# A long convolution with a gated output stage: block 1 moved behind block 0, the last chunks of the second stage reordered, two taps moved to ScalarE and GpSimd

## The chip, the cores and the metric

The kernel runs on one core of one Trainium2 chip. The metric is the time of one execution on the device in microseconds (us). The median of three runs of the kernel before is 949.27 us (947.81 to 949.87).

## The reference

For x of 8 batches, 6400 positions and 128 channels, and a filter h of 6400 positions and 128 channels, in float32:

```
Xf = rfft(x, n=2*S, axis=1);  Hf = rfft(h, n=2*S, axis=0)
y  = irfft(Xf * Hf, n=2*S, axis=1)[:, :S]        # causal long convolution, per channel
gate_pre = sum over k of conv_w[k] * y shifted by 4 - k positions   # 5 taps, per channel
out = (sigmoid(gate_pre) * (y @ w_val)) @ w_out
```

## The kernel before, in words

The kernel computes the convolution with a transform of its own, written as four sets of small matmuls, with N = 6400 = 100 x 64 positions. Forward: a transform over 100 points (`Forward.half`, weights `sd`, constants `r1_sb`, result into the tile `gy`). Second stage: 13 blocks of up to four frequencies (`s2_mm`, lines 318 to 332, constants `m2`, a ring of three slots), and behind each block the product with the filter's spectrum `h_sb`: `Product.mul_u` and `mul_t` on VectorE, `Product.add` on GpSimd (lines 350 to 371). Third stage: 16 groups of four channels, here called quads (`s3_quads`, lines 373 to 407; constants `r3_sb`, results into `dt`). Fourth: the inverse transform back to positions, `Chunk.s4`, chunk by chunk. A chunk is five of the 64 columns (chunk 60 has four), named by its first column: 0, 5, 10 up to 60.

Each chunk then passes through methods of `Chunk` (lines 433 to 555):

- `s4`: matmuls into one PSUM buffer; `copies`: ScalarE copies the result to `y`.
- The five taps of the gate, each adding scaled values into cells of the columns a to a + 4 and more. `init` (ScalarE) writes the tap that reaches a fresh column first. `keep` (ScalarE) scales tap 3 into a spare buffer `q`, and tap 2 into a buffer `r` if the chunk has one; `add` (GpSimd) adds `q` and `r` to the cells. `taps` (VectorE) adds the other taps, one `scalar_tensor_tensor` each; tap 2 is among them only if the chunk has no `r` (line 514).
- `project` (matmul with w_val), `sigm` (ScalarE), `gate` (VectorE), `output` (matmul with w_out), `store` (ScalarE copy, then a DMA on SP's queue).

The work of neighbouring batches is interleaved. In the loop over batches, line 643 runs the 16 quads of the third stage; in each quad the forward transform of the next batch (`fx.half`, into two PSUM buffers of `single()`) and steps of the chunks that the batch before left over, listed by `VALUE`, `OUTPUT` and line 632. Then line 693 runs up to 15 steps s that interleave the 13 blocks of the next batch's second stage (`s2`, `times`, two blocks in even steps and one in odd ones) with the chunks of this batch in the order `chs` (line 670). All instructions stay in program order on their engine.

What concerns the change:

- In step 0 the order on TensorE is: block 0 (line 697), transform of chunk 60 (line 699), output of a chunk left over (line 702), block 1 (line 704). `s2` also issues the load of the constants three blocks on (line 683, SP's queue), `times` the load of the spectrum four blocks on (line 690).
- The order of chunks, except in the last batch, is 60, 0, 35, 40, 45, 50, 55, 5, 10, 15, 20, 25, 30 (line 670). Chunks 25 to 55 are `late`: only `s4` and the copy are done here, and everything else in the next third stage. Chunks 10, 15 and 20 are `held`: their taps are done here, and projection, sigmoid, gate and output in the next third stage. In step s the chunk s is transformed and copied, chunk s - 1 gets its taps (VectorE), chunk s - 2 its additions (GpSimd), lines 725 to 728. Chunk 5 stands at place 7; its projection and sigmoid come in step 10, the gate at the end of step 10, the output in step 11. In step 10 the sigmoid is issued on ScalarE ahead of that step's `copies`.
- The chunks left over are handed to the next third stage in the order `cs` (line 737), so their steps of the same quad are issued in that order.
- `keep` picks `q` for chunks that are not late from four buffers `keeps`: two tiles `p_t` and the two halves of `h_sb[0]` (line 487).
- `fx.sums` (two GpSimd instructions, `sd<-x`, and a further x load on SP's queue) runs twice in the second stage, in steps 9 and 10 (line 735), unless the next batch is the last. Its first three loads are issued in step 5.
- Four PSUM buffers (`ps1`, line 612) serve `s4`, `project`, `output` and `fx.half`. Blocks and quads use two buffers of two banks each (`ps2`).

Of the kernel before, what the change touches and what calls it, by code (L numbers as in the profile page):

```python
# [17 lines left out]
N1 = 100  # L18
# [12 lines left out]
CH = 5  # L31
HEAD = (60, 4)
CHUNKS = [HEAD] + [(a, CH) for a in range(0, 60, CH)]
NCH = len(CHUNKS)
OUT_ORDER = CHUNKS[1:] + [HEAD]
LATE = 35
HELD = 10
WAIT = 25
BL = 2 * SB * C
M2B = 3  # L40
MH = 6
HB = 4
XB = 3
XH = 8
VALUE = {10: 0, 15: 1, 20: 2, 25: 4, 30: 5, 35: 6, 40: 8, 45: 10, 50: 12, 55: 14}
OUTPUT = {10: 2, 15: 3, 20: 4, 25: 6, 30: 7, 35: 8, 40: 9, 45: 11, 50: 13}
AHEAD = {
    0: (1, 0, 0), 1: (1, 0, 1), 4: (0, 0, 0), 5: (0, 0, 1), 7: (1, 1, 0), 8: (0, 1, 0),
    9: (0, 1, 1), 10: (0, 2, 0), 11: (0, 2, 1), 12: (1, 1, 1), 13: (1, 2, 0), 14: (1, 2, 1),
# [80 lines left out]
def longconv_moe(ctx: ExitStack, tc: tile.TileContext, x, h, r1, m2, r3, m4, w64, out):  # L130
# [26 lines left out]
    h_sb = [ring_at[M2B + i] for i in (2, 0, 1, 3)]  # L157
# [7 lines left out]
    p_t = [cp.tile([128, CH, N1], F32, name=f"p_{i}") for i in range(2)]  # L165
    keeps = p_t + [h_sb[0][:, i : i + CH * N1].rearrange("p (n t) -> p n t", t=N1) for i in (0, BL // 2)]
    rows = [t.rearrange("p a d n -> p (a d n)")[:, : CH * N1].rearrange("p (n t) -> p n t", t=N1) for t in sd_sb]
    hd = dp.tile([NKB, 128, 2 * SB * C], F32, name="hd")

    def weights():  # L170
# [69 lines left out]
    class Forward:  # L240


        def __init__(self, src, dst, xs=x_sb, o=0):
            self.src, self.dst, self.n, self.s, self.i, self.o = src, dst, 0, 0, 0, o
            self.xs = xs[o % len(xs) :] + xs[: o % len(xs)]
# [186 lines left out]
    class Chunk:  # L432


        def __init__(self, b, i, ch, defer):
            self.b, self.i, self.ch = b, i, ch
            a, n = ch
            self.defer = defer
            self.late = defer and WAIT <= a < HEAD[0]
            self.held = defer and HELD <= a < WAIT  # L440
            self.r = None
            self.y = yl[a][:, :n] if a >= LATE else held_y[a] if a >= HELD else dv[:, a : a + n, 0, :N1]

        def s4(self):
# [39 lines left out]
                self.p = self.y  # L484

        def keep(self):
            self.q = p_t[(self.ch[0] - HELD) // CH % 2] if self.late else keeps[(self.i + (self.i // 8 if self.defer else 1)) % 4]
            self.first(3, self.q, self.p)
            if self.r is not None:
                self.first(2, self.r, self.p)  # L490
# [129 lines left out]
    for b in range(B):  # L620
        nxt = b + 1 < B


        steps = collections.defaultdict(list)
        for c in pend:
            a = c.ch[0]
            if a == HEAD[0]:
                t = NS - 1
            else:
                t = VALUE[a]  # L630
            if c.late:
                k = (a - WAIT) // CH
                if not nxt:
                    c.r = rows[k % 3]
                steps[2 * k] += [lambda c=c: c.taps(range(2))]
                steps[2 * k + 1] += [lambda c=c: c.taps(range(2, 4)), c.add]
            steps[t] += [c.project]
            steps[t if a in OUTPUT else NS - 1] += [c.sigm, c.gate]
            if a in OUTPUT:
                steps[OUTPUT[a]] += [c.output]  # L640
                steps[OUTPUT[a] + 1] += [c.store]
        pend = [c for c in pend if c.ch[0] in (HEAD[0], HEAD[0] - CH)]
        for g in range(NS):
            e = s3_quads(4 * g)
            f = []
            if nxt:
                f = fx.half([single(), single()])
                fx.sums(nc.gpsimd)
            for u in e:
                u()  # L650
            if nxt and g in AHEAD:
                ahead(*AHEAD[g])
            for u in f:
                u(act)
            if b == 0:
                next(wgen, None)
                next(wgen, None)
                if g < 8:
                    m4_load(m4_rest[0], g % 2)
                    if g % 2:  # L660
                        m4_rest.pop(0)
            for u in steps[g]:
                u()
        if nxt:
            h_load(HB - 1)
        if b + 2 < B:
            fx = Forward(x[b + 2], gy)


        chs = CHUNKS if not nxt else sorted(CHUNKS, key=lambda c: (c != HEAD, c[0] > 0, c[0] < LATE))  # L670
        cs = [Chunk(b, i, ch, nxt) for i, ch in enumerate(chs)]
        jobs = collections.defaultdict(list)
        for i, c in enumerate(cs):
            if i and not c.late and not c.held:
                jobs[i + 3].append(c)
        if not nxt:
            jobs[NCH + 2].append(cs[0])
        pr = {}

        def s2(kb):  # L680
            if nxt and kb < NKB:
                pr[kb] = Product(kb)
                m2_load(kb + M2B)

        def times(kb):
            if kb in pr:
                pr[kb].mul_u()
                pr[kb].mul_t()
                pr.pop(kb).add()
                h_load(kb + HB)  # L690

        outs, at = [], 0
        for s in range(max(NCH, *jobs) + 2):
            kbs = list(range(at, min(at + 2 - s % 2, NKB))) if nxt else []
            at += len(kbs)
            if s == 0:
                s2(0)
            if s < 2:
                cs[s].s4()
            late = pend[s : s + 1]  # L700
            if late and s == 0:
                late[0].output()
            for kb in kbs[:1]:
                s2(kb + 1)
            if m4_rest:
                m4_load(m4_rest.pop(0))
            for c in jobs[s]:
                c.project()
            if 1 < s < NCH:
                cs[s].s4()  # L710
            for c in outs + late[: s]:
                c.output()
            for c in jobs[s]:
                c.sigm()
            for kb in kbs[:1]:
                times(kb)
            for kb in kbs[1:]:
                s2(kb + 1)
            if s < NCH:
                cs[s].copies()  # L720
            for c in outs + late:
                c.store(p_t[0][:, : c.ch[1]] if s == 0 or nxt and c.ch[0] == CH else None)
            for kb in kbs[1:]:
                times(kb)
            if 0 < s <= NCH and not cs[s - 1].late:
                cs[s - 1].taps()
            if 2 < s < NCH + 2 and not cs[s - 2].late:
                cs[s - 2].add()
            for c in jobs[s]:
                c.gate()  # L730
            outs = jobs[s]
            if b + 2 < B:
                if s == 5:
                    fx.load(XB)
                if s in (9, 10):
                    fx.sums(nc.gpsimd)
        pend = [cs[0]] + [c for c in cs if c.held or c.late]

# [44 lines left out]
```

## Time and profile before

| | us |
|---|---|
| median of 3 runs | 949.27 (947.81 to 949.87) |
| the profiled execution | 944.9 |
| its span | 943.1 |
| TensorE busy (matmuls) | 852.3 (90%) |
| VectorE busy | 746.0 (79%) |
| GpSimd busy | 579.0 (61%) |
| ScalarE busy | 510.3 (54%) |

The second stages start at 145.03, 251.38, 357.52, 466.65, 574.52, 683.84 and 793.31 us of the span, the third stages behind them at 199.14, 305.48, 411.60, 520.75, 629.05, 737.93 and 847.49.

How to read the rows: PE is TensorE, DVE VectorE, ACT ScalarE, POOL GpSimd, SP the queue that issues most DMAs. A row of the timeline gives the start in us from the span's start, the duration of the group in us, engine, line, operation, out<-in by the program's names, partitions x elements of the first instruction, the count, and in brackets the idle time of the engine ahead of it and what ended that. All lines are L117, that of the helper that records instructions, so groups are told apart by their tiles: `pt` is PSUM, `ring` holds the constants and spectra of the second stage and, later, `y`, cells and spare buffers of the chunks 10 to 30, `dt` those of the chunks 0 and 5 and the third stage's results, `gl` and `yl` those of the later chunks. On TensorE, `gy,ring` is a block (32 matmul records), `m_sb,dt` a chunk's transform (40 records), `r_sb,gy` a quad (64), `r_sb,sd` a forward half (32), and a row with `w_sb` a projection or an output (4). The chain of waits is the work that ended last, followed back from the end.

### The profile page before, as it was taken

To read this page: it belongs to the slowest core of one execution; us is meant where nothing else is said; L and a number is where in the kernel's file an instruction comes from. 1 tells how busy PE (TensorE), PEld (TensorE's weight loads), DVE (VectorE), ACT (ScalarE), POOL (GpSimd) and SP (SyncE) were. 2 spreads that over 40 slices of the span, in tenths; PEclk is the share of its full clock that TensorE was granted. 3 is DMA by queue.
4 is the path that set the end of the run, shared out by engine and by line. 5 is a ranking of instruction groups with operands and counts; after the bars stand their busy time and mean duration, and the time that the engine had idled before them with its cause. 6 is when DMAs were issued, how large, how long until landed. Compare 5 with 4: busy or idle time off the path is not lost. (4 is left out here: it accounts for less than half of the span.)

```text
span 943.1 us, 48025 instructions
## 1 busy us (share of the span) xinstructions
PE 852.3 (90%) x21360; PEld 679.1 (72%) x21360; DVE 746.0 (79%) x1041; ACT 510.3 (54%) x1222; POOL 579.0 (61%) x602
## 2 busy tenths in 40 slices
PE   7799669999999999998999999989999899999897
PEld 6699658865788568965688658865589657885563
DVE  5657658788897988888798878878787787979786
ACT  4532452278624873277624774168723685248776
POOL 5446645866477755775477764876458673864332
PEclk9999899999999999999999999999999999999999
DMA  8786547827494557826584466934586364921112
GB/s 260 255 294 230 191 155 267 298 82 216 152 322 133 167 191 238 277 81 189 164 306 152 148 194 200 312 110 153 165 284 207 114 192 149 324 88 47 66 56 97
DMA packets 79406, 177.42 MB, mean 188 GB/s; under 512 B 14048, under 2 KB 27360, under 8 KB 79200
## 3 DMA queue, kind: packets, MB, share of 16 engines
q1 hardware_dynamic: 67104, 152.33, 47.8%
q10 hardware_dynamic: 12096, 22.03, 7.9%
q8 instruction: 168, 2.75, 1.2%
q14 instruction: 38, 0.31, 0.1%
HBM read 141.56 MB, written 32.77 MB: 185 GB/s over the span
## 5 line engine op out<-in xcount | busy, mean ns | idle before, releaser
L117 POOL TENSOR_TENSOR gy<-gy,ring 128x512 f32<-128x512 f32 (+1 forms) x182 | 220.1, 1239 | 105.8 <-DVE ring L117 50.7
L117 PEld LDWEIGHTS pt<-r_sb,gy 64*64 64x64 f32 x8192 | 141.6, 136 | 107.3 <-issue 69.2
L117 DVE TENSOR_TENSOR dt<-pt,ring 128x496 f32<-128x496 f32 x256 | 159.7, 666 | 65.1 <-ACT dt L117 63.7
L117 PEld LDWEIGHTS pt<-m_sb,dt 128*64 128x64 f32 x4096 | 185.2, 136 | 28.8 <-issue 12.7
L117 PE MATMUL pt<-m_sb,dt 128*64 128x100 f32 x4096 | 193.0, 248 | 7.7 <-DVE ring L117 6.3
L117 PE MATMUL pt<-gy,ring 128*64 128x128 f32 x3008 | 189.1, 278 | 11.7 <-PE pt L117 4.2
L117 POOL TENSOR_TENSOR sd<-x 128x256 f32<-128x256 f32 x236 | 182.1, 801 | 26.2 <-issue 14.8
L117 ACT COPY ring<-pt 128x512 f32<-128x512 f32 (+2 forms) x216 | 129.2, 600 | 122.4 <-PE pt L117 58.0
L117 PEld LDWEIGHTS pt<-gy,ring 128*64 128x64 f32 x3008 | 175.0, 135 | 25.0 <-PE pt L117 13.3
L117 PE MATMUL pt<-r_sb,gy 64*64 64x64 f32 x8192 | 161.1, 225 | 19.9 <-issue 14.6
L117 PE MATMUL pt<-r_sb,sd 50*64 50x100 f32 x4608 | 137.8, 252 | 29.5 <-issue 20.0
L117 DVE TENSOR_TENSOR gy<-pt,ring 128x1024 f32<-128x1024 f32 (+1 forms) x99 | 116.9, 1181 | 54.5 <-PE pt L117 52.5
L117 DVE TENSOR_TENSOR ring<-pt,ring 128x1024 f32<-128x1024 f32 (+2 forms) x131 | 134.5, 1027 | 11.9 <-PE pt L117 2.7
L117 PEld LDWEIGHTS pt<-r_sb,sd 50*64 50x64 f32 x4608 | 114.1, 136 | 36.9 <-issue 26.9
L117 ACT COPY gy<-pt 128x400 f32<-128x400 f32 x248 | 110.6, 500 | 28.2 <-PE pt L117 27.0
L117 ACT COPY yl<-pt 128x500 f32<-128x500 f32 (+1 forms) x89 | 51.1, 574 | 128.8 <-PE pt L117 128.7
L117 POOL TENSOR_TENSOR gl<-gl,p 128x500 f32<-128x500 f32 (+1 forms) x46 | 54.1, 1177 | 103.9 <-DVE gl L117 68.7
L117 ACT COPY dt<-pt 128x16 f32<-128x16 f32 (+2 forms) x310 | 62.7, 255 | 85.8 <-PE pt L117 85.8
L117 DVE SCALAR_TENSOR_TENSOR gl<-yl,w_sb,gl 128x500 f32<-128x500 f32 (+1 forms) x107 | 92.9, 874 | 2.6 <-POOL gl L117 0.4
L117 PE MATMUL pt<-ring,w_sb 128*64 128x500 f32 x320 | 80.7, 599 | 6.9 <-DVE ring L117 6.8
L117 DVE SCALAR_TENSOR_TENSOR ring<-pt,w_sb,ring 128x500 f32<-128x500 f32 (+3 forms) x94 | 63.1, 671 | 5.7 <-ACT ring L117 1.3
L117 POOL TENSOR_TENSOR ring<-ring,p 128x500 f32<-128x500 f32 (+1 forms) x24 | 25.2, 1051 | 47.4 <-DVE ring L117 22.9
(62 smaller groups left out, 794.0 us busy)
## 6 DMA issues: line engine op xcount, KB each, us to landing
ring<-m SPq DMA_DIRECT2D x69, 512.0 KB, 5.9
ring<-hd SPq DMA_DIRECT2D x63, 512.0 KB, 5.0
x<-xl SPq DMA_DIRECT2D x118, 256.0 KB, 3.3
ring<-hd ACTq DMA_DIRECT2D x42, 256.0 KB, 3.1
ring<-m ACTq DMA_DIRECT2D x42, 256.0 KB, 3.7
out<-ring SPq DMA_DIRECT2D x40, 250.0 KB, 3.8
out<-yl SPq DMA_DIRECT2D x40, 250.0 KB, 3.2
hd<-ring SPq DMA_DIRECT2D x8, 512.0 KB, 4.8
```

Of the source, the lines that this page charges most:

```text
L117: return self._tc.keep_in_program_order(call(*args, **kwargs))
```

## The change

Block 1 is issued directly behind block 0 in step 0. The last chunks come in the order 5, 10, 25, 15, 20, 30. Chunks 10 and 15 get a buffer `r`, in the two halves of `h_sb[3]`, so that their tap 2 is made by ScalarE (`first`, one activation) and GpSimd (`add`, one addition of 128 x 500) and not by VectorE. The buffers `q` are named by a table, `KEEP`, which gives each chunk the buffer that it had. The two `fx.sums` move from steps 9 and 10 to steps 7 and 8. Since the left-over chunks follow the order `cs`, chunk 25 also stands ahead of 15 and 20 in the third stage. The last batch keeps its order.

```diff
+ORDER = (60, 0, 35, 40, 45, 50, 55, 5, 10, 25, 15, 20, 30)
+KEEP = {0: 1, 5: 3, 10: 1, 15: 2, 20: 3}
...
+    seconds = {
+        a: h_sb[HB - 1][:, i : i + CH * N1].rearrange("p (n t) -> p n t", t=N1) for a, i in ((10, 0), (15, BL // 2))
+    }
...
-            self.r = None
+            self.r = seconds.get(a) if defer else None
...
         def keep(self):
-            self.q = p_t[(self.ch[0] - HELD) // CH % 2] if self.late else keeps[(self.i + (self.i // 8 if self.defer else 1)) % 4]
+            a = self.ch[0]
+            if self.late:
+                self.q = p_t[(a - HELD) // CH % 2]
+            else:
+                self.q = keeps[KEEP[a] if self.defer else (self.i + 1) % 4]
...
-        chs = CHUNKS if not nxt else sorted(CHUNKS, key=lambda c: (c != HEAD, c[0] > 0, c[0] < LATE))
+        chs = CHUNKS if not nxt else [(a, CH) if a < HEAD[0] else HEAD for a in ORDER]
...
             if s == 0:
                 s2(0)
+                s2(1)
             if s < 2:
                 cs[s].s4()
...
             for kb in kbs[:1]:
-                s2(kb + 1)
+                if kb:
+                    s2(kb + 1)
...
-                if s in (9, 10):
+                if s in (7, 8):
                     fx.sums(nc.gpsimd)
```

## The prediction

> **What bounds the kernel now.** I read the page first: its chain of work that ended last.
>
> ```profile
> PE 27%; DVE 6%; issue 4%; ACT 2%; DMA 1%; POOL 1%; SPq 0%; DVEq 0%; POOLq 0%; ACTq 0%
> ```
>
> TensorE (PE) leads the chain and VectorE (DVE) is second, so an edit is worth what it takes from TensorE's waits, no more. The timeline shows them; I follow the batch whose second stage starts at 466.65 us. First TensorE and VectorE at the head of that stage:
>
> ```profile
> 468.55 1.54 PE L117 MATMUL pt<-m_sb,dt 128*64 128x100 f32 x32
> 469.93 0.83 PE L117 MATMUL pt<-gl,w_sb 128*64 128x400 f32 x4
> 470.60 3.86 PE L117 MATMUL pt<-gy,ring 128*64 128x128 f32 x64
> 474.29 1.90 PE L117 MATMUL pt<-m_sb,dt 128*64 128x100 f32 x40
> ```
>
> ```profile
> 472.69 1.23 DVE L117 TENSOR_TENSOR gy<-pt,ring 128x1024 f32<-128x1024 f32 x1 [1.42 <-PE pt L117]
> 473.95 1.23 DVE L117 TENSOR_TENSOR ring<-pt,ring 128x1024 f32<-128x1024 f32 x1
> 475.09 1.22 DVE L117 TENSOR_TENSOR gy<-pt,ring 128x1024 f32<-128x1024 f32 x1
> ```
>
> The first row is the inverse transform of chunk 60, the second its output projection, the 64 matmuls are blocks 1 and 2. VectorE sits idle 1.42 us until block 1 is there, then runs without a gap, and later TensorE waits for it or for what hangs on it:
>
> ```profile
> 485.06 2.07 PE L117 MATMUL pt<-gy,ring 128*64 128x128 f32 x32 [0.74 <-DVE dt L117]
> ...
> 489.28 2.07 PE L117 MATMUL pt<-gy,ring 128*64 128x128 f32 x32 [0.44 <-PE pt L117]
> ```
>
> Then TensorE at the end of the stage, where the transforms of chunks 20 and 25, the output of chunk 5, the transform of chunk 30 and the third stage follow one another:
>
> ```profile
> 512.71 1.94 PE L117 MATMUL pt<-m_sb,dt 128*64 128x100 f32 x40 [0.23 <-DVE ring L117]
> 515.13 1.94 PE L117 MATMUL pt<-m_sb,dt 128*64 128x100 f32 x40 [0.48 <-DVE ring L117]
> 518.05 1.06 PE L117 MATMUL pt<-dt,w_sb 128*64 128x500 f32 x4 [0.97 <-DVE dt L117]
> 518.93 1.89 PE L117 MATMUL pt<-m_sb,dt 128*64 128x100 f32 x40
> 520.75 1.19 PE L117 MATMUL pt<-r_sb,gy 64*64 64x64 f32 x64
> ```
>
> Three waits, 1.68 us, all for VectorE, whose rows say why: seven taps in one run, the gate of chunk 5 only behind them, then three taps of chunk 20 and 2.59 us of idleness before the third stage.
>
> ```profile
> 510.16 1.41 DVE L117 SCALAR_TENSOR_TENSOR dt<-pt,w_sb,dt 128x500 f32<-128x500 f32 x2 [0.58 <-ACT ring L117]
> ...
> 512.15 5.26 DVE L117 SCALAR_TENSOR_TENSOR ring<-pt,w_sb,ring 128x200 f32<-128x200 f32 x7
> 517.32 0.67 DVE L117 TENSOR_TENSOR dt<-pt,dt 128x500 f32<-128x500 f32 x1
> 517.91 2.28 DVE L117 SCALAR_TENSOR_TENSOR ring<-pt,w_sb,ring 128x500 f32<-128x500 f32 x3
> 522.78 1.26 DVE L117 TENSOR_TENSOR dt<-pt,ring 128x496 f32<-128x496 f32 x2 [2.59 <-ACT dt L117]
> ```
>
> **Part 1: block 1 directly behind block 0.** Nothing is added. Block 1 takes the place that chunk 60 had, near 468.5. Its data reached VectorE 472.69 - 470.60 = 2.09 us after its first matmul; so it is ready at 470.6, before VectorE is free at 472.69 - 1.42 = 471.27, and VectorE starts on it there, 1.42 us sooner. Block 2 gains nothing on TensorE, for the same work stands ahead of it: it starts half of (474.29 - 470.60) after 470.60, at 472.45, and is ready at 474.54. VectorE got to it at 475.09. The gain that VectorE keeps is thus 0.55 us. What is late next are the two waits above, 0.74 + 0.44 = 1.18 us, enough to take 0.55 in. The load of block 4's constants stands behind block 1 on SP's queue and goes out earlier; no queue entry is passed by another. Chunk 60's transform and output come later by one block; VectorE needs them only after block 2, so block 2's multiplications cover that. This happens ahead of seven third stages: 7 x 0.55 = 3.85 us.
>
> **Part 2: two taps leave VectorE, chunk 25 moves up.** Two taps of 2.28 / 3 = 0.76 us, one of chunk 10 and one of chunk 15, become each one activation and one addition. ScalarE and GpSimd (POOL) have rows for both, and for the two sums that move:
>
> ```profile
> 511.02 0.71 ACT L117 ACTIVATE p<-pt,w_sb 128x500 f32<-128x500 f32 x1
> ...
> 513.33 0.63 ACT L117 ACTIVATE dt<-dt 128x500 f32<-128x500 f32 x1
> 514.69 0.57 ACT L117 COPY ring<-pt 128x500 f32<-128x500 f32 x1 [0.73 <-PE pt L117]
> 515.16 1.44 ACT L117 ACTIVATE ring<-pt,w_sb 128x500 f32<-128x500 f32 x2
> ```
>
> ```profile
> 508.31 3.90 POOL L117 TENSOR_TENSOR gy<-gy,ring 128x512 f32<-128x512 f32 x4 [1.06 <-PE pt L117]
> 512.40 0.61 POOL L117 TENSOR_TENSOR dt<-dt,ring 128x200 f32<-128x200 f32 x1 [0.19 <-ACT ring L117]
> ...
> 515.85 1.42 POOL L117 TENSOR_TENSOR sd<-x 128x256 f32<-128x256 f32 x2
> 517.55 1.25 POOL L117 TENSOR_TENSOR ring<-ring,p 128x500 f32<-128x500 f32 x1 [0.28 <-DVE ring L117]
> ```
>
> Chunk 25 needs only a copy by ScalarE here, no VectorE. With it in the third place the transform of chunk 20 writes where chunk 25 stood, so the wait of 0.48 goes; the wait of 0.23, for chunk 5's taps, stays and now meets chunk 15.
>
> The gate of chunk 5 no longer has five taps of chunks 10 and 15 ahead of it, but two. Its sigmoid, however, gets a new wait. On GpSimd the two pairs of sums of the next batch now stand ahead of chunk 5's addition (512.40, 0.61 us): 508.31 + 3.90 + 2 x 1.42 = 515.05, so the addition ends at 515.66 and the sigmoid, before at 513.33, runs from 515.7 to 516.3. Behind it on ScalarE is queued all that chunks 15, 20 and 30 need. The gate then ends at 516.3 + 0.67 = 517.0, and chunk 5's output starts at 517.0 instead of 518.05. So the third stage starts 1.05 us earlier on TensorE, at 519.7.
>
> VectorE does not come along. Taps on a PSUM buffer start when ScalarE has finished reading it: at 510.16 they follow a wait for "ACT ring". ScalarE's steps follow each other at 0.47 us (514.69 to 515.16) to 0.7 us (half of 1.44), here taken as 0.56 for unhindered ones. From 516.2 it has seven: copy, first, keep and the new activation for chunk 15, then copy, first and keep for chunk 20: 3.9 us, to 520.1. The three taps of chunk 20 then last to 522.4, where they ended at 517.91 + 2.28 = 520.19 before. The join of the first quad, at 522.78 before, starts at 522.4: 0.4 us earlier. The 2.59 us of idle time was the cover for ScalarE's longer row, and it is used up. The x loads, two on SP behind the sums, go earlier, with nothing but the output of chunk 5 queued behind them; the new row buffers lie in the spectrum slot of block 11, which GpSimd releases at 510.8 (two of its four operations), before ScalarE gets there near 511.6. I cost these at nothing.
>
> **Where the 1.05 us goes.** In the third stage VectorE is late from the first quad to the sixth, and TensorE meets that at one place:
>
> ```profile
> 524.79 2.06 DVE L117 SCALAR_TENSOR_TENSOR ring<-ring,w_sb 128x500 f32<-128x500 f32 x2
> ...
> 528.52 0.73 DVE L117 SCALAR_TENSOR_TENSOR ring<-ring,w_sb 128x500 f32<-128x500 f32 x1
> ...
> 539.77 0.67 DVE L117 TENSOR_TENSOR ring<-pt,ring 128x500 f32<-128x500 f32 x1
> ```
>
> ```profile
> 537.92 0.87 PE L117 MATMUL pt<-r_sb,sd 50*64 50x100 f32 x32
> 540.49 1.06 PE L117 MATMUL pt<-ring,w_sb 128*64 128x500 f32 x4 [1.70 <-DVE ring L117]
> ```
>
> The projection of chunk 30 waits 1.70 us for the gate of chunk 25 (539.77, ends at 540.44), because the four single PSUM buffers are handed out in the order of their release and it gets that gate's buffer. The new order of chunks lists chunk 25 ahead of 15 and 20 in the third stage too, so its projection is issued ahead of chunk 20's output. Followed through the same rule, the gate's buffer now goes to the forward half of the sixth quad (537.92, 0.87 us), which TensorE reaches before chunk 30's projection. That half can no longer run during the wait: about 0.8 us of it falls behind the gate. If the gate moves by s, the projection moves by s + 0.8. With s = -0.4 that is +0.4: the lead of 1.05 is gone, and 0.4 with it.
>
> **The sum.** Six boundaries lead to third stages with forward halves: 6 x (0.4 - 0.55) = -0.9 us. The seventh leads into the last batch: no forward halves, no moved sums, hence no late sigmoid. There the last two waits go whole, 0.48 + 0.97 = 1.45, and part 1's 0.55: -2.0. Together -2.9 us. The profiled execution took 944.9 us (span 943.1 and 1.8 around it), 4.4 below the median of 949.27. I take the difference from the median: 946.4 us. With s from -1.0 (a ScalarE row shorter by 0.6) to 0 (a longer one) the sum runs from -6.5 to -0.5, so the forecast's own range is 942.8 to 948.8.
>
> VectorE's taps in the third stage read SBUF twice, and their price varies: 0.73 us for the one at 528.52, but 2.06 for the two at 524.79. In the sum I leave them as they are, though GpSimd's additions now end later. The Trainium skill, SBUF — State Buffer, section "Who interferes with whom", says that a VectorE instruction with two SBUF inputs and a GpSimd instruction that reads SBUF shut each other out for a whole instruction. By that rule the sum would come out slower than before; rival (d) works it out from rows.
>
> **The rivals.**
> (a) *The whole lead passes.* If the gate of chunk 25 ends before the sixth quad's half needs it, nothing is given back: 6 x (1.05 + 0.55) + 2.0 = 11.6 us, 937.7. Against it: the gate would have to come 2.5 us earlier (540.44 against 537.92), and the taps it follows do not shrink. For it: my ScalarE row may be too long, and batches whose TensorE loses time elsewhere give VectorE slack.
> (b) *Part 1 gains nothing.* The wait of 0.74 may be a load's, not VectorE's; the chain of waits has such a stretch in the next batch, a load of constants that TensorE waits for:
>
> ```profile
> 606.44 7.07 DMA ring<-m
> ```
>
> Loads that do not leave earlier hold the 0.55 back. Then 6 x 0.4 - 1.45 = +0.95: 950.2, no change that shows.
> (c) *Slower: ScalarE becomes the bound.* If its seven steps ahead of chunk 20's taps take 0.72 each (half of 1.44) instead of 0.56, they end 1.1 us later, the first join starts at 523.5 instead of 522.4, and s = +0.7: 6 x (0.7 + 0.8 - 0.55) - 2.0 = +3.7: 953.0, counting the last batch as before. It decides from s = +0.4 on, that is when chunk 20's taps end after 523.2. For it: the 1.44 us is a row of just these two steps. Against it: 514.69 to 515.16 shows that a copy gives way after 0.47.
> (d) *VectorE and GpSimd shut each other out.* GpSimd has two more additions of 1.25 and so still runs the sums of the third stage (0.71 each, half of 1.42) beside chunk 25's three taps. If each tap then waits for one whole sum, it lasts 0.73 + 0.71 = 1.44; three last 4.3 instead of 2.06 + 0.73 = 2.79, and s = -0.4 + 1.5 = +1.1: 6 x (1.1 + 0.25) - 2.0 = +6.1, 955.4. The 2.06 for two speaks against it: with sums running there already, two taps cost less than 2.88. That page of the Trainium skill would ask for it.
>
> **How the numbers follow.** The forecast has 0.50, (a) 0.16, (b) 0.15, (c) 0.15, (d) 0.03, anything else (slower, say) 0.01. A measurement of this kernel can tell about 0.2%, 1.9 us, from no change. Of the forecast's range some 0.36 lies beyond that and 0.14 within. So faster 0.36 + 0.16 = 0.52, the same 0.14 + 0.15 = 0.29, slower 0.19. The range reaches from (a), 937.5, to (c), 953.0; left out are (d), the far side of (a) and of (c).
>
> **What would show it.** Right: block 1's multiplication starts without the 1.42 us wait; chunk 20's transform has no wait; the third stage's first row comes 1 us sooner after the last block; TensorE's wait before chunk 30's projection is gone, and a longer one stands before the sixth quad's half. Wrong: no wait in that half (then (a)); the wait at the seventh block of the second stage unchanged or named a load (then (b)); the gate of chunk 25 later against the stage's start by more than 1 us (then (c), or (d) if chunk 25's taps have grown); chunk 5's sigmoid near 513.3 of this batch's clock would strike out the new wait.

## The result, and the profile after

The changed kernel is slower: 955.47 us in the median of 13 runs (950.45 to 959.31) against 949.78 of 13 runs of the kernel before (945.66 to 951.80), a ratio of 1.0062 with a 95% interval of 1.0043 to 1.0081. The forecast was 946.4, its range ended at 953.0, and slower had a chance of 0.19. The profiled execution took 950.45 us, the shortest of the 13, with a span of 948.7 us against 943.1.

I begin with the stages, each measured from its first TensorE row to the next stage's first row, the last part to the end of ScalarE's last copy. The seven second stages together are 12.7 us shorter (366.5 against 379.2), the six third stages between them 14.1 us longer (337.3 against 323.3), and the last third stage with all that is left 3.6 us longer (96.2 against 92.6). With 0.6 us at the start of the program that is the 5.6 us. So the change does what it was forecast to do where it was made, and the stage behind it gives back more.

The head of the batch that the prediction followed, TensorE and then VectorE, now with the second stage from 471.16 us:

```profile
471.16 3.91 PE L119 MATMUL pt<-gy,ring 128*64 128x128 f32 x64 [0.16 <-ACT gy L119]
474.91 1.54 PE L119 MATMUL pt<-m_sb,dt 128*64 128x100 f32 x32
...
493.25 2.07 PE L119 MATMUL pt<-gy,ring 128*64 128x128 f32 x32 [0.90 <-DVE ring L119]
```

```profile
475.69 1.21 DVE L119 TENSOR_TENSOR gy<-pt,ring 128x1024 f32<-128x1024 f32 x1
476.94 1.23 DVE L119 TENSOR_TENSOR ring<-pt,ring 128x1024 f32<-128x1024 f32 x1
479.05 1.23 DVE L119 TENSOR_TENSOR gy<-pt,ring 128x1024 f32<-128x1024 f32 x1 [0.88 <-PE pt L119]
```

Blocks 0 and 1 are one group of 64, chunk 60 comes behind them. Block 2's product starts 479.05 - 471.16 = 7.89 us into the stage, 0.55 us earlier than before (475.09 - 466.65 = 8.44), and the two waits of 0.74 and 0.44 have become one of 0.90. The end of the stage:

```profile
516.66 3.65 PE L119 MATMUL pt<-m_sb,dt 128*64 128x100 f32 x80 [0.23 <-DVE ring L119]
520.91 1.06 PE L119 MATMUL pt<-dt,w_sb 128*64 128x500 f32 x4 [0.59 <-DVE dt L119]
521.80 1.89 PE L119 MATMUL pt<-m_sb,dt 128*64 128x100 f32 x40
523.62 1.19 PE L119 MATMUL pt<-r_sb,gy 64*64 64x64 f32 x64
...
529.11 0.91 PE L119 MATMUL pt<-r_sb,sd 50*64 50x100 f32 x30 [1.34 <-ACT gy L119]
...
532.56 0.92 PE L119 MATMUL pt<-r_sb,sd 50*64 50x100 f32 x32 [0.43 <-POOL sd L119]
...
535.50 1.06 PE L119 MATMUL pt<-ring,w_sb 128*64 128x500 f32 x4 [1.04 <-DVE ring L119]
...
543.94 1.33 PE L119 MATMUL pt<-r_sb,sd 50*64 50x100 f32 x32
546.12 1.06 PE L119 MATMUL pt<-ring,w_sb 128*64 128x500 f32 x4 [0.84 <-DVE ring L119]
```

The wait of 0.48 is gone and the output of chunk 5 waits 0.59 instead of 0.97. Then the third stage, from 523.62 on, waits four times where one wait of 1.70 us stood before: for ScalarE in the half of the second quad, for GpSimd in that of the third, and for VectorE at two projections, 3.65 us in all. The half of the sixth quad (543.94), with no wait named ahead of it, takes 1.33 us where it took 0.87 before. Read backwards, all four lead to the same place. First ScalarE, then VectorE (its last row is the gate of chunk 25), then GpSimd:

```profile
519.52 0.62 ACT L119 ACTIVATE dt<-dt 128x500 f32<-128x500 f32 x1 [2.80 <-POOL dt L119]
...
528.19 0.33 ACTq L119 DMA_DIRECT2D ring<-hd  x1
528.56 0.89 ACT L119 COPY gy<-pt 128x400 f32<-128x400 f32 x2 [2.89 <-POOL ring L119]
```

```profile
520.18 0.68 DVE L119 TENSOR_TENSOR dt<-pt,dt 128x500 f32<-128x500 f32 x1 [2.02 <-ACT dt L119]
522.85 3.93 DVE L119 SCALAR_TENSOR_TENSOR ring<-pt,w_sb,ring 128x500 f32<-128x500 f32 x5 [1.99 <-POOL ring L119]
526.70 1.25 DVE L119 TENSOR_TENSOR dt<-pt,ring 128x496 f32<-128x496 f32 x2
530.00 0.68 DVE L119 TENSOR_TENSOR ring<-pt,ring 128x500 f32<-128x500 f32 x1 [2.06 <-ACT ring L119]
530.72 2.31 DVE L119 SCALAR_TENSOR_TENSOR ring<-ring,w_sb 128x500 f32<-128x500 f32 x2
...
545.40 0.67 DVE L119 TENSOR_TENSOR ring<-pt,ring 128x500 f32<-128x500 f32 x1
```

```profile
512.27 2.52 POOL L119 TENSOR_TENSOR gy<-gy,ring 128x512 f32<-128x512 f32 x2 [1.04 <-PE pt L119]
...
517.50 1.42 POOL L119 TENSOR_TENSOR sd<-x 128x256 f32<-128x256 f32 x2
518.87 0.62 POOL L119 TENSOR_TENSOR dt<-dt,ring 128x200 f32<-128x200 f32 x1
...
520.22 1.26 POOL L119 TENSOR_TENSOR ring<-ring,p 128x500 f32<-128x500 f32 x1
521.56 1.25 POOL L119 TENSOR_TENSOR ring<-ring 128x500 f32<-128x500 f32 x1
526.91 3.78 POOL L119 TENSOR_TENSOR ring<-ring 128x500 f32<-128x500 f32 x3 [4.10 <-issue]
530.65 3.67 POOL L119 TENSOR_TENSOR sd<-x 128x256 f32<-128x256 f32 x4
```

VectorE's row of five, the taps of chunks 15 and 20, waits 1.99 us for GpSimd: for the two additions of chunk 10, which end at 521.56 + 1.25 = 522.81. They share cells: chunk 10's tap 3 reaches columns 13 to 17, chunk 15's taps start at column 15. In the kernel before the taps of 15 were issued ahead of chunk 10's additions, in the same step s = 10, since taps follow their chunk by one step and additions by two. With chunk 25 put between, the taps of 15 come in step 11 and chunk 10's additions stay in step 10: the order has turned round, and with it who waits for whom. Then GpSimd in its turn waits 4.10 us (its row says "issue", but it starts 0.13 us after VectorE's row ends at 522.85 + 3.93 = 526.78): the additions of chunks 15 and 20, 3.78 us, now run inside the third stage, 3.3 us behind its start at 523.62. In the kernel before GpSimd had done them around the stage's start at 520.75:

```profile
517.55 1.25 POOL L117 TENSOR_TENSOR ring<-ring,p 128x500 f32<-128x500 f32 x1 [0.28 <-DVE ring L117]
518.75 1.42 POOL L117 TENSOR_TENSOR sd<-x 128x256 f32<-128x256 f32 x2
520.32 2.45 POOL L117 TENSOR_TENSOR ring<-ring 128x500 f32<-128x500 f32 x2
```

Everything at the head of the third stage hangs on those three additions. ScalarE's queue holds the load of the next batch's first spectrum, which overwrites the buffer `q` of chunk 15; it leaves at 528.19, behind the first of the three additions, the one that reads `q` (526.91 + 3.78 / 3 = 528.17), and the copies of the forward half stand behind it (2.89 us), which gives TensorE's 1.34. The sums that the third forward half needs stand behind the additions on GpSimd (0.43). VectorE's taps of chunk 25 (530.72) touch chunk 20's cells. They start when two things end together: the additions, at 526.91 + 3.78 = 530.69, and the gate of chunk 10 ahead of them on VectorE, at 530.00 + 0.68 = 530.68, which had waited 2.06 us for a sigmoid that stands behind ScalarE's late copies. The gates behind them are late, and two projections with them (1.04 and 0.84).

The waits that VectorE and TensorE met in the whole run of the changed kernel (total us, times, longest) show the same. First VectorE:

```profile
DVE ring L119 <- POOL ring L119: 17.0, 8, 2.9
```

```profile
PE pt L119 <- ACT gy L119: 10.0, 13, 1.3
...
PE pt L119 <- POOL sd L119: 2.6, 6, 0.4
```

The first row and the last are not among the principal waits of the kernel before, and TensorE's wait for `gy` was 2.0 us there. In the last batch there is no early sum, and the same chain stands there, TensorE first, then VectorE:

```profile
859.04 1.39 PE L119 MATMUL pt<-r_sb,gy 64*64 64x64 f32 x64 [2.32 <-DVE dt L119]
```

```profile
848.32 3.93 DVE L119 SCALAR_TENSOR_TENSOR ring<-pt,w_sb,ring 128x500 f32<-128x500 f32 x5 [2.90 <-POOL ring L119]
...
856.22 1.51 DVE L119 SCALAR_TENSOR_TENSOR ring<-ring,w_sb 128x500 f32<-128x500 f32 x2 [2.21 <-POOL ring L119]
```

### The profile page after: what moved, and what is told of

Its sections match the earlier page's. It is cut to its first block, busy times and chain, and to the rows that moved or that the text cites. A ratio compares the mean times of both kernels' runs of the same rounds, so it can differ in the third digit from the quotient of the medians.

```text
span 948.7 us, 48047 instructions
## 1 busy us (share of the span) xinstructions
PE 856.2 (90%) x21360; PEld 681.4 (72%) x21360; DVE 739.8 (78%) x1027; ACT 514.4 (54%) x1236; POOL 604.9 (64%) x616
## 5 line engine op out<-in xcount | busy, mean ns | idle before, releaser
L119 POOL TENSOR_TENSOR sd<-x 128x256 f32<-128x256 f32 x236 | 191.2, 840 | 25.5 <-issue 13.0
L119 PE MATMUL pt<-r_sb,sd 50*64 50x100 f32 x4608 | 142.0, 255 | 32.9 <-issue 12.9
L119 PEld LDWEIGHTS pt<-r_sb,sd 50*64 50x64 f32 x4608 | 116.8, 138 | 43.1 <-issue 19.8
L119 PE MATMUL pt<-ring,w_sb 128*64 128x500 f32 x320 | 82.9, 606 | 11.2 <-DVE ring L119 11.1
L119 DVE SCALAR_TENSOR_TENSOR ring<-pt,w_sb,ring 128x500 f32<-128x500 f32 (+3 forms) x80 | 52.8, 660 | 20.1 <-POOL ring L119 14.8
L119 POOL TENSOR_TENSOR ring<-ring 128x500 f32<-128x500 f32 (+1 forms) x38 | 43.9, 1163 | 36.7 <-issue 20.5
```

Of the source, the lines that this page charges most:

```text
L119: return self._tc.keep_in_program_order(call(*args, **kwargs))
```

## The experiments

Each kernel was timed against the kernel before on the same chip; ratios are to that. Stage lengths come from the profiled execution of each, as above: the mean of seven second stages, the mean of six third stages, and the last part. Third stages of one kernel differ by up to 3 us (52.0 to 55.4 in the kernel before), for TensorE also pauses where the trace names no releaser, so their means vary by some tenths. The profiled executions of the kernel before, of the changed one and of the early block alone lie 4.4 to 5.0 us below their medians, the others within 3.5: the lengths say where time goes, the ratios how much.

| kernel | ratio (95%) | second | third | last |
|---|---|---|---|---|
| before | 1 | 54.17 | 53.88 | 92.59 |
| changed | 1.0062 (1.0043 to 1.0081) | 52.36 | 56.22 | 96.22 |
| early block alone | 0.9963 (0.9942 to 0.9983) | 53.49 | 53.33 | 92.50 |
| changed, sums back | 1.0077 (1.0051 to 1.0103) | 51.65 | 57.07 | 95.79 |
| changed, no buffer r | 1.0035 (1.0019 to 1.0051) | 52.26 | 56.58 | 94.63 |
| changed, old order of left-over chunks | 1.0078 (1.0054 to 1.0103) | 52.25 | 56.93 | 95.74 |
| changed, additions 10 behind taps 15 | 1.0000 (0.9977 to 1.0023) | 52.32 | 55.85 | 94.94 |
| changed, loads two quads later | 1.0072 (1.0045 to 1.0099) | 52.45 | 57.04 | 96.10 |
| early block, new order | 1.0071 (1.0047 to 1.0096) | 51.62 | 58.01 | 94.35 |
| early block, r | 0.9874 (0.9837 to 0.9911) | 52.22 | 54.38 | 92.56 |
| changed, old order of chunks | 0.9882 (0.9843 to 0.9921) | 52.45 | 53.74 | 92.61 |
| r alone | 0.9947 (0.9925 to 0.9969) | 52.70 | 54.47 | 92.69 |
| early block, r for 10 only | 0.9949 (0.9925 to 0.9972) | 52.69 | 54.51 | 92.69 |
| early block, r for 5, 10, 15 | 1.0029 (1.0000 to 1.0059) | 53.03 | 55.79 | 93.43 |
| changed, additions 10 late, sums back | 0.9948 (0.9923 to 0.9972) | 51.64 | 55.81 | 94.91 |
| changed, chunk 25 one place up | 0.9979 (0.9953 to 1.0005) | 52.61 | 55.43 | 94.53 |

The theory that I started from, G, was that GpSimd's additions of chunks 15 and 20 come too late. Its rivals were S, the moved sums that hold up chunk 5's sigmoid (2.80 us in the rows above), and L, chunk 25 ahead of 15 and 20 in the third stage.

**The early block alone**, the kernel before with one edit:

```diff
                 s2(0)
+                s2(1)
...
-                s2(kb + 1)
+                if kb:
+                    s2(kb + 1)
```

> The kernel before with one part of the change: block 1 directly behind block 0. All theories on the slowdown (G: GpSimd's additions for chunks 15 and 20 come too late; S: the moved sums hold up chunk 5's sigmoid; L: chunk 25 stands ahead of 15 and 20 in the third stage) lay nothing to this part. The prediction's part 1 gives 0.55 us ahead of each of seven third stages: 3.85 us faster, a ratio of 0.996. If part 1 does nothing, the ratio is 1.000; if it costs, above 1.002.

It gained 0.37%, 3.5 us of 946.31; the forecast's term was 3.85. The second stages are 0.5 to 1.2 us shorter. The loss is in the rest of the change.

**The sums back in their old steps**, the changed kernel otherwise:

```diff
-                if s in (7, 8):
+                if s in (9, 10):
```

> The changed kernel with the two sums back in steps 9 and 10. S: chunk 5's sigmoid comes about 2.5 us earlier, ScalarE's row with it, and the time falls to that of the kernel before or below (950 or less). G: the taps of chunk 15 still wait for the additions of chunk 10, which now have a sum ahead of them, so the additions of 15 and 20 end no earlier: 952 to 957, no more than 0.5 us gained per boundary. L: no change, 955.

No gain, so S does not hold as the cause. Chunk 5's output no longer waits and the second stage is 0.7 us shorter, but the third is 0.9 us longer. VectorE and GpSimd in this kernel show why; the stage begins at 525.47:

```profile
525.69 3.93 DVE L119 SCALAR_TENSOR_TENSOR ring<-pt,w_sb,ring 128x500 f32<-128x500 f32 x5 [4.28 <-ACT p L119]
```

```profile
524.40 1.26 POOL L119 TENSOR_TENSOR ring<-ring 128x500 f32<-128x500 f32 x1
```

The sums have moved in front of chunk 10's additions, which now end at 524.40 + 1.26 = 525.66, and the taps of chunk 15 start 0.03 us later. The row names ScalarE as the releaser, but the time shows that it was GpSimd: one queue's delay was exchanged for another's.

**No buffer r**, the changed kernel otherwise:

```diff
-            self.r = seconds.get(a) if defer else None
+            self.r = None
```

> The changed kernel with the two taps given back to VectorE (no buffer r): ScalarE and GpSimd lose two steps of 0.7 and 1.25 us, VectorE gains two of 0.76. G: the three additions of 15 and 20 become two, the last ends about 1.7 us earlier against the start of the third stage, and VectorE's taps of chunk 25 with it: 6 x 1.5 = 9 us less than the changed kernel, about 946. S and L: the sums and the order are untouched, so 955, or more by the taps that VectorE gets back.

The direction is G's, the size is far from it: 0.27% of gain against the changed kernel, with intervals that overlap. The last addition does end 1.5 us earlier, at 5.5 us into the stage for 7.1, as G asked. But the first begins hardly earlier, at 3.1 us for 3.3, and ScalarE's load, which needs only the first, leaves at 4.4 us for 4.6. The taps of chunk 15 wait only half as long for others, but VectorE has both taps back.

**The left-over chunks in their old order in the third stage:**

```diff
-        pend = [cs[0]] + [c for c in cs if c.held or c.late]
+        pend = [cs[0]] + sorted((c for c in cs if c.held or c.late), key=lambda c: (c.ch[0] < LATE, c.ch[0]))
```

> The changed kernel with the left-over chunks handed on in the old order (10, 15, 20, 25, 30), the order within the second stage unchanged. L: the wait of 1.04 us before chunk 20's projection goes in six third stages and the sixth quad's wait changes place: 949 or less. G: VectorE is as late as before and TensorE only waits for it elsewhere: 953 to 956.

No gain: L falls. In the same batch the waits at the projections of chunks 20 and 30 change from 1.04 and 0.84 us to 0.38 and 1.85; the other two stay at 1.33 and 0.43.

What was left was the order itself. The next four runs took it apart, with a new rival R: that the added buffer's own work is the loss.

**GpSimd's additions of chunk 10 put behind VectorE's taps of chunk 15:**

```diff
-            if 2 < s < NCH + 2 and not cs[s - 2].late:
+            if nxt and s == 11:
+                cs[8].add()
+            elif 2 < s < NCH + 2 and not cs[s - 2].late and not (nxt and s == 10):
                 cs[s - 2].add()
```

> The changed kernel, with one thing put back: GpSimd's two additions of chunk 10 are issued behind VectorE's taps of chunk 15, as in the kernel before, and not ahead of them. Theory G, made narrower by the runs so far: putting chunk 25 between 10 and 15 moved the taps of chunk 15 behind the additions of chunk 10, whose cells they share; in the trace of the changed kernel VectorE stands 1.99 us there, and the chain from there (taps 15, taps 20, additions 15, additions 20, taps 25, load of the next spectrum) runs 1.3 to 3 us too far into the third stage. Then this kernel starts the taps of chunk 15 some 1.2 to 1.8 us earlier; the PE waits of 1.34 us (half of the second quad) and 1.04 us (projection of chunk 20) shrink to some tenths each, the wait at chunk 30's projection grows by about 0.5 us: -1.7 us in each of seven stages, ratio to the kernel before 0.994 (0.991 to 0.999). Rival R, the added buffer's own work on ScalarE and GpSimd (two scaled copies, two additions) is the loss: nothing of it is taken away here, ratio 1.006 as for the changed kernel.

0.6% of the loss is undone, with no work taken away; 0.994 was not reached. VectorE and GpSimd of this kernel, whose third stage starts at 524.39:

```profile
523.12 3.94 DVE L119 SCALAR_TENSOR_TENSOR ring<-pt,w_sb,ring 128x500 f32<-128x500 f32 x5 [1.50 <-ACT ring L119]
```

```profile
526.13 5.00 POOL L119 TENSOR_TENSOR ring<-ring 128x500 f32<-128x500 f32 x4
```

The taps no longer wait for GpSimd, but for ScalarE's three scaled copies of chunk 15, which stand behind chunk 5's late sigmoid and end at 523.09. They start 1.27 us ahead of the stage (0.77 in the changed kernel), and the last addition still ends 6.7 us behind its start (7.1). The additions put back bring waits of their own: a ScalarE copy waits 1.76 us for GpSimd, until the second of them ends (527.41), and VectorE's first join 1.12 us for ScalarE (528.18).

**The two loads on ScalarE's queue two quads later:**

```diff
-    0: (1, 0, 0), 1: (1, 0, 1), 4: (0, 0, 0),
+    2: (1, 0, 0), 3: (1, 0, 1), 4: (0, 0, 0),
```

> The changed kernel, with the two loads of the next batch's first spectrum, which ScalarE's queue issues in quads 0 and 1 of the third stage, issued in quads 2 and 3. In the changed kernel the first of them holds ScalarE for 2.9 us, since it overwrites the buffer that chunk 15's first addition reads. Theory G, ScalarE's part of it: the PE wait of 1.34 us at the half of the second quad goes, up to 9 us over seven stages. Theory G, VectorE's part: the taps of chunk 25 and all joins and gates behind them still wait for the additions of chunk 20, so PE loses the time at the projection of chunk 20 instead. I take 1.001 as the ratio (0.997 if ScalarE's queue alone was the cause, 1.005 if VectorE's chain bounds). Rival R: 1.006, no change.

No gain. The wait of 1.34 us goes from every third stage, and in its place the half of the third quad waits 1.63 us for the sums instead of 0.43:

```profile
538.76 0.92 PE L119 MATMUL pt<-r_sb,sd 50*64 50x100 f32 x32 [1.63 <-POOL sd L119]
```

```profile
536.94 2.30 DVE L119 SCALAR_TENSOR_TENSOR ring<-ring,w_sb 128x500 f32<-128x500 f32 x2 [2.21 <-POOL ring L119]
```

The second row is VectorE's taps of chunk 25. The gate of chunk 10 comes 2.1 us sooner here than in the changed kernel, and the taps wait for the additions all the same, to the same 7.1 us behind the stage's start (529.82). So ScalarE's stop alone is not what costs: with it gone, what GpSimd still has to do holds TensorE and VectorE as long. I had taken 1.001, with 1.005 if VectorE's chain bounds; 1.0072 (from 1.0045) lies nearer to R's number, though not for R's reason, as the next two runs show.

**The early block and the new order, without r and with the sums in their old steps** (the changed kernel with the edits of the second and third run together):

> The kernel before with the early block and the new order of the chunks alone: no second buffer, the sums in their old steps. Theory G: the taps of chunk 15 stand behind chunk 10's addition here too, and the additions of 15 and 20 come after the third stage's start: ratio 1.004 (1.002 to 1.008), against 0.9963 of the kernel with the early block alone. Rival R: the order costs nothing, 0.996 to 0.998.

The order alone costs 1.1% over the early block: 1.0071 lies near the upper end of what G had put down, and R falls. VectorE, with the third stage at 528.57:

```profile
528.22 4.70 DVE L119 SCALAR_TENSOR_TENSOR ring<-pt,w_sb,ring 128x500 f32<-128x500 f32 x6 [2.93 <-POOL ring L119]
```

This kernel has one of the shortest second stages, 51.6 us, and the longest third, 58.0. The order lets TensorE out of the second stage 1.9 us earlier, while VectorE and GpSimd come later: what it removes is not work but the overlap of it.

**The early block and r, in the old order, with the sums in their old steps:**

```diff
+    seconds = {
+        a: h_sb[HB - 1][:, i : i + CH * N1].rearrange("p (n t) -> p n t", t=N1) for a, i in ((10, 0), (15, BL // 2))
+    }
...
-            self.r = None
+            self.r = seconds.get(a) if defer else None
```

> The kernel before with the early block and the second buffer alone (one tap each of chunks 10 and 15 by ScalarE and GpSimd), in the old order, the sums in their old steps. Theory G: taps 15 are issued ahead of chunk 10's additions, so VectorE waits for none of them; GpSimd ends its additions 2.5 us later, at 4.5 us into the third stage where VectorE's taps of chunk 25 began at 4.0: some tenths lost in each stage, ratio 0.998 (0.995 to 1.000). Rival R: the added work is the loss: 1.002 to 1.006.

0.9874, beyond what both theories had put down: r is worth 0.9% here. TensorE and GpSimd, with the third stage at 518.67:

```profile
515.96 1.06 PE L117 MATMUL pt<-dt,w_sb 128*64 128x500 f32 x4 [0.30 <-DVE dt L117]
```

```profile
519.69 3.80 POOL L117 TENSOR_TENSOR ring<-ring 128x500 f32<-128x500 f32 x3
```

The wait of 0.48 is gone here too, without the new order, and the output of chunk 5 waits 0.30. The same three additions start 1.0 us behind the stage's start, not 3.3, and the third stage is 54.4 us long (53.3 with the early block alone, 56.2 in the changed kernel).

**The changed kernel with the old order of chunks and all the rest of the change:**

```diff
-        chs = CHUNKS if not nxt else [(a, CH) if a < HEAD[0] else HEAD for a in ORDER]
+        chs = CHUNKS if not nxt else sorted(CHUNKS, key=lambda c: (c != HEAD, c[0] > 0, c[0] < LATE))
```

> The changed kernel with the old order of the chunks and everything else of the change kept (early block, second buffer, sums at steps 7 and 8). Theory G (the order is the whole of the loss): taps 15 stand ahead of chunk 10's additions again, ratio 0.988 (0.985 to 0.992), as with the second buffer and the early block alone (0.9874); the earlier sums cost nothing. Rival S', the earlier sums cost something too where GpSimd's additions are otherwise on time, since chunk 5's sigmoid stands some 2.8 us behind them: 0.995 (0.993 to 0.998).

0.9882: the order is the whole loss, 1.8% between this kernel and the changed one. The sums' place matters for nothing that can be told here, so S' falls. GpSimd of this kernel, whose third stage starts at 520.97:

```profile
521.24 3.80 POOL L119 TENSOR_TENSOR ring<-ring 128x500 f32<-128x500 f32 x3 [0.89 <-issue]
```

The additions start 0.3 us behind the stage's start: 3.0 us sooner than in the changed kernel, and only the order differs.

**r alone, in the kernel before** (the edit above that adds `seconds`, without the early block):

> The kernel before with the second buffer alone: no early block, old order, old steps of the sums. If the two parts add up (0.9874 against 0.9963 with the early block, that is 0.9% for the second buffer), the ratio is 0.991 (0.988 to 0.994). Rival, the one that the prediction's sum stood on: what VectorE gains is given back in the third stage, and the second buffer pays only together with the early block: 0.998 (0.996 to 1.000).

0.9947, between the two: r pays by itself, 0.5%. Whether it pays more with the early block (0.9%) the intervals leave open.

**r for chunk 10 only, with the early block:**

```diff
-a, i in ((10, 0), (15, BL // 2))
+a, i in ((10, 0),)
```

> The early block and the second buffer, in the old order, the second buffer for chunk 10 alone. VectorE's taps of 10 and of 15 both stand ahead of the gate of chunk 5, on which the output of chunk 5 waits. If VectorE's row of steps to that gate is what pays, each of the two chunks is worth half of the 0.9%: 0.992 (0.989 to 0.995). If GpSimd's longer additions cost something that the gain hides, one addition fewer brings it nearer to 0.9874: 0.988.

0.9949, less than the half that was expected, though the interval reaches to 0.9925. By the profiles the two are about alike: chunk 5's output and the transforms ahead of it wait 1.69 us with the early block alone (0.23, 0.48 and 0.98), 1.14 with the buffer for chunk 10 (0.23 and 0.91) and 0.53 with both.

**r for chunk 5 as well, in `p_t[0]`:**

```diff
+    seconds[5] = p_t[0]
```

> The early block and the second buffer, in the old order, with a second buffer for chunk 5 as well (a third tap moved from VectorE to ScalarE and GpSimd). In the trace of the kernel with chunks 10 and 15 alone the output of chunk 5 waits only 0.30 us for its gate, so VectorE has at most that to gain there, 2 us over seven stages; against it GpSimd's additions become longer by some 1.4 us in each stage, and ScalarE's row by 0.7 us ahead of chunk 10's copies. Forecast 0.988 (0.985 to 0.992), no gain over 0.9874; if VectorE's row still were the bound, 0.982.

Slower than the kernel before by 0.3%, with an interval that just reaches 1, and 1.5% behind the kernel with two buffers: a third one more than eats up what two gained, and I had looked for no change. TensorE and ScalarE of this kernel:

```profile
519.60 1.06 PE L117 MATMUL pt<-dt,w_sb 128*64 128x500 f32 x4 [1.02 <-DVE dt L117]
...
543.10 1.31 PE L117 MATMUL pt<-ring,w_sb 128*64 128x500 f32 x4 [1.84 <-DVE ring L117]
```

```profile
518.21 0.62 ACT L117 ACTIVATE dt<-dt 128x500 f32<-128x500 f32 x1 [1.08 <-POOL dt L117]
```

Chunk 5's sigmoid now waits 1.08 us for the longer additions of its own chunk, and the output that needs it waits 1.02 us again. How the 1.5% divides between these waits no run separates.

Open was the 1.2% between 1.0000 (additions of 10 late) and 0.9882 (old order). **Additions of 10 late and the sums back**, both edits together:

> The changed kernel with chunk 10's additions behind chunk 15's taps (as in the run before that reached 1.000) and also the sums back at steps 9 and 10. Open is the 1.2% between that run and the old order (0.988). Theory P: what remains is the place itself; the transforms of chunks 15 and 20 stand one chunk later on TensorE, so ScalarE's copies, VectorE's taps and GpSimd's additions of both come later whatever the queues do: ratio 1.000 (0.998 to 1.004), no gain. Theory Q: what remains is chunk 5's sigmoid, which stood 2.8 us behind the earlier sums and held up ScalarE's row for chunk 15; without it the taps of chunk 15 start up to 1.5 us earlier in seven stages: 0.992 (0.989 to 0.996).

0.9948: Q is the larger part, half a per cent. Alone, putting the sums back had gained nothing, since chunk 10's additions then stood behind them; with those out of the way it does gain. The rest I put down to P, though no run takes it apart: in the trace ScalarE now waits for TensorE before it can copy chunk 15, which is transformed one chunk later.

```profile
520.93 0.57 ACT L119 COPY ring<-pt 128x500 f32<-128x500 f32 x1 [1.02 <-PE pt L119]
```

**Chunk 25 moved by one place and not two:**

```diff
-ORDER = (60, 0, 35, 40, 45, 50, 55, 5, 10, 25, 15, 20, 30)
+ORDER = (60, 0, 35, 40, 45, 50, 55, 5, 10, 15, 25, 20, 30)
```

> The changed kernel with chunk 25 moved by one place and not by two: 5, 10, 15, 25, 20, 30. The taps of chunk 15 then stand ahead of chunk 10's additions again, but the taps of chunk 20 stand behind chunk 15's two additions. Theory P (each place that a chunk with taps is moved back costs): chunk 20 alone comes later, about half of the loss of 1.8%: 0.997 (0.994 to 1.000). Theory G with its chain alone: VectorE waits for two additions of 2.5 us once and later than in the changed kernel, but only chunk 20's one addition is left behind it: 0.991 (0.987 to 0.994).

0.9979, P's number: about half of the loss. But it is again G's turned order that VectorE shows, this time with the taps of chunk 20 behind chunk 15's additions:

```profile
524.20 2.28 DVE L119 SCALAR_TENSOR_TENSOR ring<-pt,w_sb,ring 128x500 f32<-128x500 f32 x3 [4.69 <-POOL ring L119]
```

The number is P's and the row G's, so this run does not tell the two apart. By the runs above, roughly: of the 1.8%, 0.6% came back by the order of issue alone, 0.5% more by the sums on top of it, and 0.7% stays, which fits the place but is not shown to be its doing.

Both kernels with r in the old order beat the kernel before and the changed one: 0.9874 and 0.9882, whose difference is within their intervals.

## Why the prediction was wrong, point by point

**Part 1, right.** Block 2's product starts 7.89 us into the stage, as worked out (474.54 - 466.65), and the part alone is worth 3.5 us (1.6 to 5.5 by its interval) for a term of 3.85. Rival (b) is out.

**The end of the second stage, right.** Counted from block 11's first product on GpSimd (508.31 before, 512.27 after), chunk 5's sigmoid was forecast at 7.4 us and came at 7.25, the third stage at 11.4 and came at 11.35. The new wait behind the sums is there, and the third stage comes 1.09 us earlier on this clock (12.44 before), for a forecast of 1.05: second stages of 52.4 us against 53.5 with the early block alone.

**VectorE's way to the first join, near, and partly by luck.** It was forecast at 14.1 us on this clock and came at 14.4. ScalarE's seven steps set the time in the forecast, and they ended as forecast (523.94, that is 11.7 us on this clock for 11.8). But VectorE waited 1.99 us for GpSimd's additions of chunk 10, a wait that the forecast does not have. It cost the join only some 0.5 us, because ScalarE's row would have held the taps of chunk 20 until nearly the same time.

**The step that failed** is the one behind it: "In the sum I leave them as they are, though GpSimd's additions now end later." I had weighed the later additions only as a neighbour that slows taps down, not as work that others wait for. They end 7.1 us into the third stage, and ScalarE's queue, the sums, chunk 25's taps and through them two projections wait for them. So the taps of chunk 25 start 7.1 us into the stage where they started at 4.04, and the gate of chunk 25 ends at 545.40 + 0.67 = 546.07, 22.45 us into the stage where it ended at 19.69: 2.8 us later, where the forecast had 0.65 (a lead of 1.05 less 0.4).

The path was wrong with it. The lead was to be given back at one place, the sixth quad's half, which was to get the PSUM buffer of that gate. The trace shows that the projection of chunk 30 still follows the gate (546.12, behind 546.07), and that no wait stands ahead of the half (543.94), though it takes 0.46 us longer. The time went at three places ahead of it and one behind it. The forecast's sign for "no wait in that half" pointed to rival (a), which is wrong too.

**The sizes.** Six boundaries were forecast at -0.15 us each (0.4 - 0.55) and came at +0.6 (14.1 us longer third stages, 10.2 us shorter second stages, over six): 4.8 us of the miss. The last batch was forecast at -2.0; its second stage gained 2.5, but the three additions came late there as well, and the last part lost 3.6: 3.1 us. I had said of that batch that it has no late sigmoid and counted both waits as gained; it has the turned order all the same. The start of the program gave the remaining 0.6 us.

**The rivals.** (c) decides from a first join at 14.9 us on the clock above, and it came at 14.4. (d) has a mechanism that is there, at a price that is not. It asks for 2.9 us for two taps beside sums; the row at 530.72 has 2.31, and the kernel before had 2.06 already, so the taps of chunk 25 add 0.25 us and not 1.5. The prediction read that 2.06 as two taps beside sums; in the trace only one of the two met a sum (last section). That (d)'s 955.4 lies beside the measured 955.47 is chance. So slower stood in the list only under mechanisms that do not make the loss: the additions as a dependence were no rival at all, though the methods' order in the steps (taps one step behind, additions two) stood in the code.

## What to carry to other kernels

Before a chunk is moved past another, list for every cell that two engines update in place which of them is issued first, before and after: a moved step can turn that order round, and the engine that now comes second waits for the whole queue ahead of the other. A stage's end is not over when its busiest engine leaves it: count the engine that finishes last there, and what the next stage hangs on. A change of several parts should be timed part by part, for here one that is worth -0.4% and one that is worth -0.9% lay hidden under one of +1.8%.

## What the runs showed of the hardware

VectorE's taps with both inputs in SBUF and GpSimd's sums take turns. In the last batch, where no sum ran, two such taps took 1.51 us (856.22), 0.74 each. In the third stage of the changed kernel, instruction by instruction:

```profile
530.65 0.73 POOL L119 TENSOR_TENSOR sd<-x 128x256 f32<-128x256 f32 x1
...
530.72 1.20 DVE L119 SCALAR_TENSOR_TENSOR ring<-ring,w_sb 128x500 f32<-128x500 f32 x1
...
531.34 1.17 POOL L119 TENSOR_TENSOR sd<-x 128x256 f32<-128x256 f32 x1
...
531.95 1.08 DVE L119 SCALAR_TENSOR_TENSOR ring<-ring,w_sb 128x500 f32<-128x500 f32 x1
```

They overlap in time, but they end in turn, 0.5 to 0.6 us apart: sum 531.38, tap 531.92, sum 532.51, tap 533.03. A sum that starts beside a tap takes 1.17 us instead of 0.73. In the kernel before, the first of the two taps at 524.79 met a sum and took 1.28 us, the second met none and took 0.74. The Trainium skill, SBUF — State Buffer, section "Who interferes with whom", calls this an exclusive lock between a VectorE instruction with two SBUF inputs and a GpSimd instruction that reads SBUF. The order of the ends agrees with that; the added time, 0.34 to 0.54 us a tap, is less than a whole sum.

A releaser in a row is to be read with the clock in hand: "ACT p" was named for 4.28 us that ended 0.03 us behind GpSimd's addition, and "issue" for 4.10 us that ended 0.13 us behind VectorE's taps.
